# Exchange between partition quarters on VectorE, slice 13's cast on ACT, and VectorE's work that waits for ACT behind the gap's lower part

## Chip, cores and metric

One core of a Trainium2 chip. The metric is the device time of one execution in microseconds, the median of several. A profile is of one execution; its span runs from the first to the last instruction.

## What is computed

Agent attention and then a gated feed-forward layer, all in float32, B = 4, N = 12480 tokens, C = 128 channels, 49 agents, 2048 hidden columns:

```python
def sm(a, b):
    s = scale * (a @ b.transpose(0, 2, 1))      # scale = 1 / sqrt(128)
    e = np.exp(s - s.max(-1, keepdims=True))
    return e / (e.sum(-1, keepdims=True) + 1e-09)
agent_v = sm(agents, k) @ v
x = (sm(q, agents) @ agent_v).reshape(B * N, C)
h = x @ w_in
out = (h * (1.0 / (1.0 + np.exp(-1.702 * h)))) @ w_out
```

## The kernel before

**Groups, slices, gaps.** The tokens are cut into 52 groups of 960 (n = 0 to 51, 13 to a batch, two halves of 480), the hidden columns into 16 slices of 128. For a group n and a slice f (u = 16 n + f) the kernel does: `up`, products of the query weights (agent values times w_in) into two PSUM banks `ph`; ACT's gelu of both halves into `g`; `high`, g rounded to float32r, `gh`; `low`, VectorE's gl = g - gh; `down`, three products of (gh, gl) with the high and low part of w_out, added up in two banks `po`. Products are done in pairs, one on the upper and one on the lower 64 rows of the array.

**The cast in `high`** has two makers (`by_dma`): for even slices and those in `BY_DMA` a DMA that POOL issues, one gap later (`late`); for the others ACT, at the end of the same gap (`soon`). `low` runs three slices behind `up`; `down` of slice f stands in the group's own gaps f and f + 1, five and six gaps behind its `up`. There are 5 buffers of g, 7 of gh and 5 of gl, and 4 banks of `ph`, so two slices.

**The order by hand.** The whole program is a list of gaps, 17 to a group (`GAPS`), written out in `gap`: first the jobs put at that gap, then `up` of one slice, `low` of the slice three back, the `down` products, and last the `high` of the slices that are due. Gap k of group n holds `up` of slice k - 1 + 6 counted from group n, so the group's own slices 6 to 15 go up in its gaps 1 to 10 and the next group's 0 to 5 in gaps 11 to 16. Each engine runs its instructions in this order; a job put at a gap stands in front of that gap's `low` on VectorE and of its gelu on ACT.

**Jobs.** Beside the feed-forward work of one batch run the next batch's keys, then its values, then its weights, and always the query attention of the groups ahead. Key scores of a slice of keys take two gaps from the places in `K_AT` (even groups 2, 8, 14; odd groups 4, 11), values one gap from `V_AT` (even 6, 13; odd 3, 9, 15). All of these and the query scores share one tile of two banks, `ps_m`. Two gaps behind the key scores `key_store` has ACT copy one part of the banks to `score`, VectorE add the other to it and VectorE take the running maximum. A value tile is cast to `v_pair` by a DMA that POOL issues (`value_high`), five gaps ahead of its product.

**Query softmax.** The scores of two groups lie in `e` as blocks of 32 agents by tokens, with the 49 agents in two neighbouring quarters of the partitions. So the maximum (`query_max`) and the sum (`query_sums`) of a quarter have to be joined with those of its neighbour: `exchange` makes four copies of 32 x 30 from `m` or `z` to `x`, each to the other quarter. The one of maxima is put at gap 7 of an even group, after `query_max` at 5 and before `query_shift` at 12; the one of sums at gap 4 of the odd group, before `query_recip` at 6. `query_back` writes p at gaps 6 and 12, `query_high` (ACT, q_hi) and `query_low` (VectorE, q_lo = p - q_hi) follow at 9 and 15.

**What shares what.** POOL's queue holds the exchanges, the gh casts and the v_pair casts; SP's queue the loads (keys, values, queries) and the stores. VectorE's order in a gap is jobs, then `low`.

Of the kernel before, what the change touches and what calls it, by code (L numbers as in the profile page):

```python
# [18 lines left out]
TB = 120  # L19
KB = 8  # L20
# [7 lines left out]
GAPS = 17  # L28
E_AT = 0
BL = 32  # L30
A0 = 25
K_AT = ((2, 8, 14), (4, 11))
V_AT = ((6, 13), (3, 9, 15))
PAIR = 2 * 128 + 16
BY_DMA = (5, 13)
EARLY = 3
EPS = 1e-09

# [2 lines left out]
def kernel(  # L41
# [10 lines left out]
    nc = tc.nc  # L52
# [225 lines left out]
    def by_bank(t):  # L278
        return t.rearrange("p (c j) a -> p c j a", c=2)
# [29 lines left out]

    def key_store(g, s):  # L310
        out = by_bank(score[:TB, g * KB : (g + 1) * KB, :])
        if isinstance(s, tuple):
            nc.scalar.copy(out=out, in_=s[0])  # L313
            nc.vector.tensor_add(out=out, in0=s[1], in1=out)  # L314
            s = out
        else:
            nc.scalar.copy(out=out, in_=s)
        running_max(g, s)

    def key_max_0(d):  # L320
# [361 lines left out]
            scores_exact(b, kts.pop((b, g)), columns(banks[b, g][0]))  # L682

    def do_key_store(b, g):
        key_store(g, banks.pop((b, g))[1])

    def do_key_values(b, g):
        sums[b, g] = key_values(g)
# [15 lines left out]
    def do_query_max(k):  # L704
        tops[k] = query_max(k)
        others[k] = small("x")

    def do_exchange(k, of, quarters, by):
        exchange(of[k], others[k], quarters, by)

    def do_query_shift(k):
        query_shift(k, tops.pop(k), others.pop(k))
# [193 lines left out]
    def put(t, fn):  # L906
        at.setdefault(t, []).append(fn)
# [12 lines left out]
    for n in range(B * NG):  # L920
        t = LAG + n * GAPS
        m = n + 1
        runs = [(t, n + 3)] if n else [(t + 3, 2), (t + 11, 3)]
        for at_, q in runs:
            if q < B * NG:
                take(at_, 1)
                put(at_, lambda q=q: do_query_scores(q))
                put(at_ + 1, lambda q=q: do_query_turn(q))
            if q > 2:
                put(at_ + 2, lambda q=q: do_query_load(q + 1))  # L930
        k = n // 2 + 1
        if n % 2 == 0 and k < B * NG // 2:
            put(t + (5 if n else 13), lambda k=k: do_query_max(k))
            put(t + (12 if n else 15), lambda k=k: do_query_shift(k))
            put(t + GAPS, lambda k=k: query_exp(k))
            put(t + GAPS + 2, lambda k=k: do_query_sums(k))
            put(t + GAPS + 6, lambda k=k: do_query_recip(k))
            for i in range(2):
                quarters = (2 * i, 2 * i + 1)
                put(t + (7 if n else 14), lambda k=k, q=quarters: do_exchange(k, tops, q, nc.gpsimd.tensor_copy))  # L940
                put(t + GAPS + 4, lambda k=k, q=quarters: do_exchange(k, sums, q, nc.gpsimd.tensor_copy))
                put(t + GAPS + (6, 12)[i], lambda k=k, i=i: do_query_back(k, i))
                put(t + GAPS + (9, 15)[i], lambda m=n + 2 + i: do_query_high(m))
                put(t + GAPS + (9, 15)[i], lambda m=n + 2 + i: do_query_low(m))
    put(0, lambda: do_query_load(3))
    put(LAG + 1, lambda: do_query_back(0, 1))
    put(LAG + 3, lambda: do_query_high(1))
# [22 lines left out]
    for b in range(B - 1):  # L970
        begin = gap_of(b * NG * NF) + (0 if b else 7)
        end = gap_of((b + 1) * NG * NF)
        slots = [LAG + n * GAPS + k for n in range(B * NG) for k in K_AT[n % 2]]
        slots = [t for t in slots if t >= begin + 4][:NKG]
        if not b:
            exact.update(((1, 0), (1, 1)))
        for k, t in enumerate(slots):
            if (b + 1, k) not in exact:
                wide.add((b + 1, k))
            put(max(t - 13, first_free[k] if k < 3 and not b else 0), lambda b=b, k=k: do_key_load(b + 1, k))  # L980
            for i in range(4):
                put(t - 4 + i, lambda b=b, k=k, i=i: do_key_split(b + 1, k, i))
            take(t, 2)
            put(t, lambda b=b, k=k: do_key_scores(b + 1, k, 0))
            put(t + 1, lambda b=b, k=k: do_key_scores(b + 1, k, 1))
            put(t + 2, lambda b=b, k=k: do_key_store(b + 1, k))
        mx = {}
        put(t + 2, lambda mx=mx: key_max_0(mx))
        t = free(t + 3)
        put(t, lambda mx=mx: key_max_1(mx))  # L990
        t = free(t + 2)
        put(t, lambda mx=mx: key_max_2(mx))
        shift = t + 1

        n0 = (shift + 1 - LAG - E_AT + GAPS - 1) // GAPS
        places = [(n, i) for n in range(n0, B * NG) for i in V_AT[n % 2] if i > 5 or n > n0]
        for k, (n, i) in enumerate(places[:NKG]):
            t = LAG + n * GAPS + i
            exp_at = LAG + (n if i > 5 else n - 1) * GAPS + E_AT
            exps.setdefault(exp_at, []).append(k)  # L1000
            put(min(shift + 3 * k, exp_at - 1), lambda k=k: key_shift(k, nc.vector.tensor_tensor))
            put(t - 16, lambda b=b, k=k: do_value_load(b + 1, k))
            put(t - 5, lambda b=b, k=k: value_high(vts[b + 1, k]))
            put(t - 2, lambda b=b, k=k: value_low(vts.pop((b + 1, k))))
            put(t - 4, lambda k=k: key_pair(k))
            take(t, 1)
            put(t, lambda b=b, k=k: do_key_values(b + 1, k))
            put(t + 1, lambda b=b, k=k: do_key_sum(b + 1, k))
        w = {}
        put(t + 2, lambda b=b, w=w: weights_0(accs.pop(b + 1), w))  # L1010
        t = free(t + 3)
        put(t, lambda w=w: weights_1(w))
        for c in range(0, F // 512, 2):
            t = free(t + 2)
            assert t < end + 4 * c - 3, (b, begin, shift, end, t)
            put(t, lambda b=b, w=w, c=c: weights_parts(b + 1, w, c))
# [43 lines left out]
    def gap(t):  # L1060
        n, k = divmod(t - LAG, GAPS)
        final = n == B * NG - 1
        if t < LAG:
            u = t if t < LAG - 1 else None
        elif final:
            u = n * NF + LAG + k
        elif k == 0:
            u = LAG - 1 if n == 0 else None
        else:
            u = n * NF + LAG + k - 1  # L1070
        before, late[:] = list(late), []
        rest()
        for job in at.pop(t, ()):
            job()
        if u is not None:
            if u < total:
                do_up(u)
                rest()
            if k != NF:
                for i in low_of(u):  # L1080
                    do_low(i)
        if t >= LAG:
            do_downs(n, k)
        if u is not None and k == NF:
            for i in low_of(u):
                do_low(i)
        for u in before + soon:
            do_high(u)
        soon.clear()
        if k == 2 or final:  # L1090
            send()
# [57 lines left out]
```

## Time and profile before

| | |
|---|---|
| median of 3 runs | 1913.1 us (1912.54 to 1915.93) |
| the profiled execution | 1913.12 us |
| its span | 1911.3 us |
| PE busy | 1877.3 us (98%) |
| VectorE (DVE) busy | 1452.1 us (76%) |
| ACT busy | 1369.4 us (72%) |
| POOL busy | 455.1 us (24%) |
| mean granted TensorE clock | 0.997 |

Busy time is the time in which an engine has an instruction running. PE's matmuls are pipelined and their ends are modelled, so a PE that is busy 98% need not be at its peak; a stop shows better in the distance between the starts of two products. The other engines' shares are means over stages that differ: keys, values and weights come in turn, and in the last 14 groups there is nothing of them. So the rows below are taken by group.

### The profile page before, as it was taken

The page shows a single profiled execution, that of the slowest core. Times are in us where ns is not written, and L with a number is a line of the kernel's source. Part 1 is how long each engine was busy: PE and PEld are TensorE (multiplying, and loading weights), DVE is VectorE, ACT ScalarE, POOL GpSimd, SP SyncE. Part 2 cuts the span into 40 slices and gives each one's busy share as a digit, 9 for nine tenths or more (in the row PEclk, how much of TensorE's full clock was granted, in tenths as well). Part 3 has the DMA queues.
Part 4 walks back from the last instruction along what each step waited for, and adds up shares of the span by engine and source line. Part 5 has one row for each costly group of instructions (what it writes and reads, how often), then busy time and mean ns, then how long its engine had stood idle before and what let it go on. Part 6 is the DMA issues. An engine that isn't in the chain of part 4 may idle for free.

```text
span 1911.3 us, 46738 instructions
## 1 busy us (share of the span) xinstructions
PE 1877.3 (98%) x18872; PEld 1666.2 (87%) x18872; DVE 1452.1 (76%) x1826; ACT 1369.4 (72%) x2314; POOL 455.1 (24%) x822
## 2 busy tenths in 40 slices
PE   8999999999999999999999999999999999999999
PEld 8699988888888998887888999988888888898897
DVE  7888788787678887886877887787876666676664
ACT  4677677777676677776776776866767777777775
POOL 0113323223223212222212232232221122212111
PEclk9999999999999999999999999999999999999999
DMA  9465558788556556887755554888974545555444
GB/s 366 165 218 200 193 176 238 223 236 219 175 188 207 197 177 207 222 251 215 213 185 186 200 197 167 229 215 208 240 195 166 193 171 190 183 175 186 161 167 151
DMA packets 158979, 384.63 MB, mean 201 GB/s; under 512 B 15699, under 2 KB 73235, under 8 KB 158763
## 3 DMA queue, kind: packets, MB, share of 16 engines
q0 software_dynamic: 115152, 273.82, 46.2%
q1 hardware_dynamic: 43611, 107.83, 17.7%
q8 instruction: 148, 2.42, 0.6%
q14 instruction: 68, 0.56, 0.1%
HBM read 82.25 MB, written 25.56 MB: 56 GB/s over the span
## 4 chain that ended last, share of the span: by engine, by line
PE 84%; issue 5%; DVE 5%; DMA 4%; POOL 2%; ACT 1%; POOLq 0%; DVEq 0%; SPq 0%
PE po L216 50%; PE ph L216 26%; PE ps_m L216 4%; DMA gh<-g 3%; PE ps_m L470 2%; DVE gl L592 1%; PE ph L292 1%; POOL x L494 1%; PE ps_m L428 1%; PE po L614 0%; ACT g L573 0%; DVE rest L197 0%; POOL gh L585 0%; DVE score L355 0%; DVE m L503 0%
## 5 line engine op out<-in xcount | busy, mean ns | idle before, releaser
L573 ACT ACTIVATE g<-ph 128x480 f32<-128x480 f32 x1664 | 853.7, 570 | 468.9 <-PE ph L216 414.1
L592 DVE TENSOR_TENSOR gl<-g,gh 128x960 fp32r<-128x960 f32 x832 | 936.7, 1150 | 220.7 <-DMA gh<-g 165.3
L216 PE MATMUL po<-gh,wo_h 64*128 64x480 f32 x3300 | 722.4, 381 | 4.7 <-DMA gh<-g 2.5
L216 PE MATMUL po<-gl,wo_h 64*128 64x480 f32 x3300 | 715.1, 379 | 7.3 <-DVE gl L592 7.2
L216 PE MATMUL po<-gh,wo_l 64*128 64x480 f32 x3300 | 708.1, 375 | 0.0
L585 POOL DMA_DIRECT2D gh<-g x518 | 276.8, 534 | 1358.4 <-ACT g L573 1106.6
L216 PEld LDWEIGHTS po<-gh,wo_h 64*128 64x128 f32 x3300 | 388.3, 184 | 55.4 <-ACT o L622 25.1
L216 PEld LDWEIGHTS po<-gl,wo_h 64*128 64x128 f32 x3300 | 388.5, 186 | 37.7 <-DVE gl L592 12.4
L216 PEld LDWEIGHTS po<-gh,wo_l 64*128 64x128 f32 x3300 | 387.5, 184 | 25.7
L216 PE MATMUL ph<-q_hi,wh 56*128 56x480 f32 x1664 | 369.8, 391 | 0.4 <-ACT wh L433 0.3
L216 PE MATMUL ph<-q_lo,wh 56*128 56x480 f32 x1664 | 359.2, 378 | 0.0
L216 PE MATMUL ph<-q_hi,wl 56*128 56x480 f32 x1664 | 358.1, 377 | 0.3 <-DVE wl L434 0.3
L587 ACT CAST gh<-g 128x960 fp32r<-128x960 f32 x311 | 310.4, 998 | 9.8
L216 PEld LDWEIGHTS ph<-q_hi,wh 56*128 56x128 f32 x1664 | 196.0, 184 | 25.8 <-ACT g L573 5.8
L216 PEld LDWEIGHTS ph<-q_hi,wl 56*128 56x128 f32 x1664 | 195.2, 185 | 14.2 <-DVE wl L434 1.0
L216 PEld LDWEIGHTS ph<-q_lo,wh 56*128 56x128 f32 x1664 | 197.1, 187 | 10.4
L494 POOL COPY x<-m 32x30 f32<-32x30 f32 x100 | 90.6, 906 | 33.0 <-DVE m L503 29.3
L314 DVE TENSOR_TENSOR score<-ps_m,score 120x392 f32<-120x392 f32 x37 | 20.9, 564 | 69.7 <-ACT score L313 62.6
L548 DVE TENSOR_TENSOR q_lo<-p,q_hi 120x480 fp32r<-120x480 f32 x52 | 34.2, 657 | 48.3 <-ACT q_hi L542 48.3
L216 PE MATMUL ps_m<-ag_part,rest 64*128 64x49 bf16 (+1 forms) x1184 | 59.0, 192 | 4.4 <-DVE rest L197 4.1
L372 DVE TENSOR_TENSOR v_pair<-vt,v_pair 120x1024 fp32r<-120x1024 f32 x39 | 47.4, 1216 | 20.6 <-DMA v_pair<-vt 20.6
L624 DVE COPY o<-po 128x480 f32<-128x480 f32 x37 | 24.3, 657 | 50.9 <-PE po L216 46.6
(136 smaller groups left out, 1288.6 us busy)
## 6 DMA issues: line engine op xcount, KB each, us to landing
gh<-g POOLq DMA_DIRECT2D x518, 480.0 KB, 3.3
kt<-kT SPq DMA_DIRECT2D x52, 480.0 KB, 4.0
outT<-o SPq DMA_DIRECT2D x104, 240.0 KB, 4.2
qt<-qT SPq DMA_DIRECT2D x49, 480.0 KB, 4.4
vt<-v SPq DMA_DIRECT2D x39, 512.0 KB, 6.6
v_pair<-vt POOLq DMA_DIRECT2D x39, 480.0 KB, 6.0
vt<-v SPq DMA_DIRECT2D x13, 480.0 KB, 6.4
words<-w_in SPq DMA_DIRECT2D x4, 512.0 KB, 8.7
```

The lines of the kernel that those rows point to most:

```text
L216: ins = nc.tensor.matmul(tile_position=(c * H, 0), **kw)
L292: nc.tensor.matmul(out=ps[:TB, j * 2 * A : (j + 1) * 2 * A], lhsT=kt[:, c * KB // 2 + j, :], rhs=ag_key.rearrange("p b a -> p (b a)"), sta ...
L314: nc.vector.tensor_add(out=out, in0=s[1], in1=out)
L372: nc.vector.tensor_sub(out=vp[:TB, :, C : 2 * C], in0=vt[:TB], in1=vp[:TB, :, 0:C].bitcast(F32))
L470: nc.tensor.matmul(out=ps[c * H : (c + 1) * H, i * n : (i + 1) * n], lhsT=ag_sb[:, b, :], rhs=x[:, t : t + n], start=True, stop=True, tile ...
L494: by(out=x[to * BL : (to + 1) * BL], in_=t[i * BL : (i + 1) * BL])
L548: nc.vector.tensor_sub(out=q_lo[r], in0=p[r], in1=q_hi[r].bitcast(F32))
L573: nc.scalar.activation(out=g[:, c, :], in_=ph[c][:, :CH], func=AF.Gelu_apprx_sigmoid)
L585: nc.gpsimd.dma_start(out=gh, in_=g)
L587: nc.scalar.copy(out=gh, in_=g)
L592: nc.vector.tensor_sub(out=gl, in0=g, in1=gh.bitcast(F32))
L624: nc.vector.tensor_copy(out=o, in_=po[c][:, :CH])
```

## The change

The four calls of `exchange` for a pair of groups (eight copies) go from POOL's `tensor_copy` to VectorE's. Slice 13 leaves `BY_DMA`, so that ACT casts it. The third place for keys in even groups goes from gap 14 to 13. `key_store` keeps ACT's copy alone; VectorE's add and running maximum go to `key_rest`. A second list of jobs, put at half gaps (t + 0.5), runs behind the gap's `low` and `down`; `key_rest`, the first step of the key maximum and `query_low` are put there. In the even groups `query_max` goes from gap 5 to 4, the exchange of maxima from 7 to 6, `query_shift` from 12 to 9; `query_high` from 9 and 15 to 8 and 14.

```diff
--- before.py
+++ after.py
@@ -29,10 +29,10 @@
 E_AT = 0
 BL = 32
 A0 = 25
-K_AT = ((2, 8, 14), (4, 11))
+K_AT = ((2, 8, 13), (4, 11))
 V_AT = ((6, 13), (3, 9, 15))
 PAIR = 2 * 128 + 16
-BY_DMA = (5, 13)
+BY_DMA = (5,)
 EARLY = 3
 EPS = 1e-09
 
@@ -309,12 +309,13 @@
 
     def key_store(g, s):
         out = by_bank(score[:TB, g * KB : (g + 1) * KB, :])
+        nc.scalar.copy(out=out, in_=s[0] if isinstance(s, tuple) else s)
+
+    def key_rest(g, s):
+        out = by_bank(score[:TB, g * KB : (g + 1) * KB, :])
         if isinstance(s, tuple):
-            nc.scalar.copy(out=out, in_=s[0])
             nc.vector.tensor_add(out=out, in0=s[1], in1=out)
             s = out
-        else:
-            nc.scalar.copy(out=out, in_=s)
         running_max(g, s)
 
     def key_max_0(d):
@@ -682,7 +683,10 @@
             scores_exact(b, kts.pop((b, g)), columns(banks[b, g][0]))
 
     def do_key_store(b, g):
-        key_store(g, banks.pop((b, g))[1])
+        key_store(g, banks[b, g][1])
+
+    def do_key_rest(b, g):
+        key_rest(g, banks.pop((b, g))[1])
 
     def do_key_values(b, g):
         sums[b, g] = key_values(g)
@@ -930,18 +934,18 @@
                 put(at_ + 2, lambda q=q: do_query_load(q + 1))
         k = n // 2 + 1
         if n % 2 == 0 and k < B * NG // 2:
-            put(t + (5 if n else 13), lambda k=k: do_query_max(k))
-            put(t + (12 if n else 15), lambda k=k: do_query_shift(k))
+            put(t + (4 if n else 13), lambda k=k: do_query_max(k))
+            put(t + (9 if n else 15), lambda k=k: do_query_shift(k))
             put(t + GAPS, lambda k=k: query_exp(k))
             put(t + GAPS + 2, lambda k=k: do_query_sums(k))
             put(t + GAPS + 6, lambda k=k: do_query_recip(k))
             for i in range(2):
                 quarters = (2 * i, 2 * i + 1)
-                put(t + (7 if n else 14), lambda k=k, q=quarters: do_exchange(k, tops, q, nc.gpsimd.tensor_copy))
-                put(t + GAPS + 4, lambda k=k, q=quarters: do_exchange(k, sums, q, nc.gpsimd.tensor_copy))
+                put(t + (6 if n else 14), lambda k=k, q=quarters: do_exchange(k, tops, q, nc.vector.tensor_copy))
+                put(t + GAPS + 4, lambda k=k, q=quarters: do_exchange(k, sums, q, nc.vector.tensor_copy))
                 put(t + GAPS + (6, 12)[i], lambda k=k, i=i: do_query_back(k, i))
-                put(t + GAPS + (9, 15)[i], lambda m=n + 2 + i: do_query_high(m))
-                put(t + GAPS + (9, 15)[i], lambda m=n + 2 + i: do_query_low(m))
+                put(t + GAPS + (8, 14)[i], lambda m=n + 2 + i: do_query_high(m))
+                put(t + GAPS + (8.5, 14.5)[i], lambda m=n + 2 + i: do_query_low(m))
     put(0, lambda: do_query_load(3))
     put(LAG + 1, lambda: do_query_back(0, 1))
     put(LAG + 3, lambda: do_query_high(1))
@@ -984,8 +988,9 @@
             put(t, lambda b=b, k=k: do_key_scores(b + 1, k, 0))
             put(t + 1, lambda b=b, k=k: do_key_scores(b + 1, k, 1))
             put(t + 2, lambda b=b, k=k: do_key_store(b + 1, k))
+            put(t + 2.5, lambda b=b, k=k: do_key_rest(b + 1, k))
         mx = {}
-        put(t + 2, lambda mx=mx: key_max_0(mx))
+        put(t + 2.5, lambda mx=mx: key_max_0(mx))
         t = free(t + 3)
         put(t, lambda mx=mx: key_max_1(mx))
         t = free(t + 2)
@@ -1084,6 +1089,8 @@
         if u is not None and k == NF:
             for i in low_of(u):
                 do_low(i)
+        for job in at.pop(t + 0.5, ()):
+            job()
         for u in before + soon:
             do_high(u)
         soon.clear()
```

## Rows read from the trace of the kernel before

**Rows 1.** The page's head line.
```profile
span 1911.3 us, 46738 instructions
```
**Rows 2.** Stretches of one group each: length, busy us (instructions) by engine, clock, DMA; tail, even value, even key, odd value.
```profile
1553.83:1586.53 32.70, 32.70 (x298) 28.01 (x296) 23.73 (x29) 25.91 (x44) 6.41 (x14) 1.00 0.52 182
...
433.39:468.30 34.91, 34.91 (x332) 31.27 (x329) 25.62 (x31) 26.01 (x43) 10.33 (x17) 1.00 0.88 226
864.32:905.16 40.84, 37.62 (x330) 32.41 (x328) 26.55 (x32) 26.02 (x43) 10.33 (x17) 0.96 0.79 219
sum 301.29, PE 288.17 PEld 248.28 DVE 217.50 ACT 208.28 POOL 83.17; mean PE 36.02 PEld 31.03 DVE 27.19 ACT 26.04 POOL 10.40
...
649.48:686.59 37.11, 37.11 (x492) 34.52 (x490) 29.92 (x39) 24.80 (x44) 10.52 (x17) 1.00 0.59 205
212.61:251.22 38.61, 37.18 (x492) 34.61 (x489) 29.88 (x39) 24.75 (x44) 12.65 (x17) 1.00 0.53 184
sum 263.88, PE 260.21 PEld 241.21 DVE 209.05 ACT 173.31 POOL 85.68; mean PE 37.17 PEld 34.46 DVE 29.86 ACT 24.76 POOL 12.24
...
828.76:864.32 35.56, 35.56 (x346) 32.41 (x344) 30.67 (x39) 27.52 (x46) 9.01 (x17) 1.00 0.84 236
sum 215.63, PE 214.56 PEld 194.79 DVE 188.34 ACT 164.97 POOL 55.71; mean PE 35.76 PEld 32.47 DVE 31.39 ACT 27.49 POOL 9.29
```
**Rows 3.** Timeline of PE: start and length in us, operation, count [idle before, releaser].
```profile
372.66 0.49 PE L216 MATMUL po<-gl,wo_h 64*128 64x480 f32 x2 [0.81 <-DVE gl L592]
...
876.77 0.49 PE L216 MATMUL po<-gh,wo_h 64*128 64x480 f32 x2
878.06 0.49 PE L216 MATMUL po<-gl,wo_h 64*128 64x480 f32 x2 [0.80 <-DVE gl L592]
...
889.53 0.39 PE L216 MATMUL po<-gh,wo_l 64*128 64x480 f32 x2
891.05 0.48 PE L216 MATMUL po<-gh,wo_h 64*128 64x480 f32 x2 [1.14 <-DMA gh<-g]
892.35 0.49 PE L216 MATMUL po<-gl,wo_h 64*128 64x480 f32 x2 [0.81 <-DVE gl L592]
...
1393.23 0.49 PE L216 MATMUL po<-gl,wo_h 64*128 64x480 f32 x2 [0.47 <-DVE gl L592]
```
**Rows 4.** A stretch of 2 us, columns as in rows 2: the clock is third from the end.
```profile
895.00:897.00 2.00, 2.00 (x14) 1.93 (x12) 2.00 (x3) 0.74 (x2) 0.00 (x0) 0.50 0.00 0
```
**Rows 5.** Timeline of POOL in groups n = 4 and n = 22.
```profile
224.62 7.20 POOL L494 COPY x<-m 32x30 f32<-32x30 f32 x4
...
878.98 2.58 POOL L494 COPY x<-m 32x30 f32<-32x30 f32 x4 [4.03 <-DVE m L503]
881.51 0.96 POOL L368 DMA_DIRECT2D v_pair<-vt  x1
882.46 1.09 POOL L585 DMA_DIRECT2D gh<-g  x2
```
**Rows 6.** The exchange's copies, whole run: count, ns min/median/max, first and last start.
```profile
L494 POOL COPY x<-m x100: 200/208/6460, 93.2 to 1794.5; 32x30 f32<-32x30 f32 x100
L494 POOL COPY x<-z x100: 200/207/1699, 109.0 to 1820.6; 32x30 f32<-32x30 f32 x100
...
L494 DVE COPY x<-z x4: 170/174/176, 47.4 to 47.9; 32x30 f32<-32x30 f32 x4
```
**Rows 7.** The page's groups: count, busy us, mean ns, idle us before, its releasers.
```profile
L592 DVE TENSOR_TENSOR gl<-g,gh 128x960 fp32r<-128x960 f32 x832 | 936.7, 1150 | 220.7 <-DMA gh<-g 165.3
...
L587 ACT CAST gh<-g 128x960 fp32r<-128x960 f32 x311 | 310.4, 998 | 9.8
...
L314 DVE TENSOR_TENSOR score<-ps_m,score 120x392 f32<-120x392 f32 x37 | 20.9, 564 | 69.7 <-ACT score L313 62.6
```
**Rows 8.** The gh casts that POOL issues, whole run, columns as in rows 6.
```profile
L585 POOL DMA_DIRECT2D gh<-g x518: 528/531/732, 62.2 to 1896.6; - x173
...
DMA to landing us min/median/max: 2.8/3.3/9.8
```

## The prediction

> **What bounds the kernel now.** I read the span first [rows 1], then the stretches of one token group each, then the stops of PE inside them, then what PE's releasers had waited for. In a group of the tail, where neither keys nor values are done beside the feed-forward work, PE is busy for 32.70 of 32.70 us [rows 2]: there it is the bound and nothing else can be late. With work beside it a group has a floor as well, the cheapest group of the same make: 34.91 us for an even group with two value slices, 37.11 for an even one with three key slices, 35.56 for an odd one with three value slices [rows 2]. In these PE is busy throughout too. So all that an edit off PE can win is what groups of the same make take over their floor:
> - eight even value groups (n = 6, 8, 10, 20, 22, 32, 34, 36): 301.29 - 8 x 34.91 = 22.0 us;
> - seven even key groups: 263.88 - 7 x 37.11 = 4.1 us;
> - six odd value groups: 215.63 - 6 x 35.56 = 2.3 us [rows 2].
>
> The dearest is n = 22 with 40.84 us [rows 2]. It has two stops. In the **second**, PE's pair at 889.53 is followed by one at 891.05 that waits for a DMA into gh, and that by one at 892.35 that waits for VectorE's gl [rows 3]; pairs come every 0.22 us when nothing is late (a down product is one such pair), so 1.3 + 1.1 us are lost. Two microseconds later the granted clock is 0.50, which is 1.2 GHz, with PE busy all the while [rows 4]; it had stood still for most of the 2.5 us behind 889.9. The rest of the 5.9 us over the floor is that slower stretch and the slices behind it. Why was gh late? POOL did the exchange x<-m from 878.98 for 2.58 us, then the issue for v_pair at 881.51, and only then two gh casts, at 882.46 [rows 5]: slices 12 and 13, one behind the other. In the key group n = 4 the same exchange took 7.20 us [rows 5]. The copies themselves are short: the median is 208 ns, the longest 6460 ns (x<-m) and 1699 ns (x<-z) [rows 6]. The **first** stop, 876.77 and 878.06 [rows 3], comes before any exchange of its group: gh of slice 6 landed late among query load, output stores and value load. Five of the eight groups have it, from 372.66 to 1393.23 [rows 3]; read like the second one, by the gaps between starts, they cost 1.4, 1.5, 1.3, 0.9 and 1.0 us, 6.1 in all; a small one (0.3 us) lies in the floor group too.
>
> **The change part by part.** *Exchange.* 50 exchanges (25 of x<-m, 25 of x<-z) leave POOL, four copies each. On VectorE one copy takes 174 ns [rows 6], taken as 0.77 us for four with the small gaps between them: 50 x 0.77 = 38.5 us more VectorE time. They lie beside PE's work. The exchange of maxima stands in gap 6 of an even group, ahead of low for slice 8; the one of sums in gap 4 of an odd group, ahead of low for slice 6. VectorE is busy for 217.50 / 8 = 27.2 us of an even value group, 29.9 of the even key floor, 188.34 / 6 = 31.4 of an odd value group [rows 2], so the time is there (32.2 of 35.6 in the tightest). Where VectorE waits for a DMA into gh anyway, the exchange of sums falls into that wait. I take nothing on the path, and 38.5 us as the far bound. What POOL gets back is its place in the queue: slice 12's issue is no longer behind an exchange of 2.6 to 7.2 us, and v_pair's, put at gap 8, is no longer behind it either, so it runs some microseconds before the gh casts and not into them.
>
> *A page against it.* One gh issue took 732 ns where the median is 531 [rows 8]. The Trainium skill (SBUF — State Buffer, Who interferes with whom) says that a VectorE copy in its two-port mode holds the port pair that it shares with GpSimd, and that GpSimd can't write DMA descriptors meanwhile: the four new copies would delay an issue. By the trace that is 0.2 us at most in 518 issues, and by the copies' own length 0.77 us an exchange; against 2.6 to 7.2 us before, the sum stays as it is by either.
>
> *Slice 13 by ACT.* 52 casts of 998 ns [rows 7] are 51.9 us more on ACT, 52 issues of 531 ns [rows 8] less on POOL, and 52 of the 518 gh transfers [rows 8] less. The cast stands at the end of gap 8, behind that slice's two gelus, between the DMA slices 12 and 14. ACT is busy for 27.5 of 35.9 us in the odd value groups [rows 2], so 28.5 fit; in gap 8 of an odd group, with q_hi moved there as well, it has more than a gap's work and is behind by less than 1 us until gap 9, which has one slice's gelus alone. The two slices of ph that PE may run ahead cover that; without them it would be on PE's path. Taken: 0; bounds: 0 and 0.6 us in each of 26 odd groups, 16 us. What it gives back: in the second stop's burst (v_pair, 12, value load, 13, 14) a gh landing took up to 9.8 us against a median of 3.3 [rows 8]; one of five transfers goes, and v_pair moves out in front of it.
>
> *VectorE's work behind the lows.* key_rest and q_low go behind the gap's low. Now VectorE stands before them for ACT, 69.7 us before the key add, most of it for ACT's score copy [rows 7], with a low (1.15 us) queued behind it. What is queued behind the wait afterwards is only the next gap's work. Nothing of this is counted as PE time, since no stop that I read has it as its last cause; it pays for VectorE's new 38.5 us. Who waits: the bank of ps_m is free later, by one low, 1.15 us. Its next taker comes two gaps later or more (key slot 13, store at 15, query scores at 17), 3.9 us: covered. With the slot left at 14 it would not be. key_max_0 moves behind the low too, ahead of a transpose of PE in the next gap, three times in all: between -1 and +1.15 us each, since the low comes before it where the wait for ACT stood; I take 0.
>
> *Earlier places.* Max 5 to 4, shift 12 to 9, q_hi 9 to 8 and 15 to 14: the same instructions; the maximum now comes before low of slice 6, where VectorE waits for that gh in the first stop, so it no longer lies in the catch-up behind it. I count nothing.
>
> **The sum.** The first stops are no work of the change: 22.0 - (6.1 - 5 x 0.3) = 17.4 us can go in even value groups, 4.1 in even key groups (all behind the exchange), 2.3 in odd value groups (gh of slice 8 stood behind x<-z). 17.4 + 4.1 + 2.3 = 23.8. Span 1911.3 - 23.8 = 1887.5; the profiled execution is 1.8 us longer than its span and agrees with the median (1913.12 and 1913.1), so **1889 us**.
>
> **The rivals.**
> *A, the burst stays.* The landing is late for the transfers' own sake, and only POOL's lateness goes: in n = 22 slice 12 is issued about 1.1 us earlier, 7 groups x 1.1 = 7.7, and 4.1 + 2.3 as above: 14.1, hence 1899 us. For it: landings up to 9.8 us [rows 8]. Against it: v_pair leaves the burst, and a transfer with it.
> *B, the first stops go too.* With the maximum ahead of them and less traffic: 6.1 us more, 1883. Against it: nothing that feeds slice 6's transfer changes.
> *C, slower: VectorE's queue.* Place: gaps 4 to 8, where one engine in order has exchange, sums or shift and the lows. PE waits as soon as a low ends later than the start of its gl product; in the odd value groups that is where VectorE already has 31.4 us of work. If every exchange outside the 14 or so of the tail, where VectorE is busy for 23.73 of 32.70 us [rows 2], came onto the path, it were 36 x 0.77 = 27.7 us against 23.8 won: 1917 us. It decides from 31 of these 36 on. Against it: 69.7 us of waiting leave the same queue.
> *D, no change: ps_m.* The stops go, and PE stops instead at the next taker of the bank: 39 slices x 0.6 us (half a low) = 23.4. Against it: the takers lie two gaps away.
>
> **How the numbers follow.** Forecast 0.67, A 0.17, B 0.05, D 0.05, C 0.06. The measurement can tell about 0.2%, 3.8 us. Forecast, A and B are faster: 0.89; same 0.05; slower 0.06. The range takes in forecast, A and B with a margin of 2 us: 1881 to 1901; it leaves C and D out.
>
> **What will show it.** Right, step by step: no COPY on POOL, 208 on VectorE of about 0.17 us; POOL's issue of slice 12 some 0.3 us behind its gelu; 466 gh transfers; n = 22 and n = 32 within 1.5 us of 35 us, no stretch at 0.50 inside; the key group n = 4 at 37.1; VectorE's wait for ACT's score far under 62 us; first stops still there. Wrong if the gap between starts at 889 only shrinks (A), if tail groups leave 32.7 us, if PE waits for VectorE in gaps 4 to 8 of groups that stood at their floor (C), or before query or key scores (D).

## The result and the profile after

The change takes 1890.3 us (median; 1888.5 to 1891.4) against 1914.5 of the kernel before in the same series: 24.2 us less, a ratio of 0.9872 [0.9855, 0.9890]. The forecast was 1889. The profiled execution of after took 1891.41 us, its span is 21.7 us shorter than the one of [rows 1], and PE is busy for 99% of it. Head and first section of its page:

```profile
span 1889.6 us, 46586 instructions
PE 1869.7 (99%) x18872; PEld 1677.2 (89%) x18872; DVE 1490.3 (79%) x2026; ACT 1418.8 (75%) x2366; POOL 293.3 (16%) x570
```

VectorE has 38.2 us more to do and ACT 49.4 us more, POOL 161.8 us less. That answers which engine does the work, not where the time was won. For this the stretches of one group each, as in [rows 2]: length, busy us (instructions) by engine, clock, DMA share, GB/s; a tail group, two even value groups (n = 22 and 32) with the sum of eight, an even key group (n = 4) with the sum of seven, two odd value groups (n = 21 and 23) with the sum of six:

```profile
1532.09:1564.77 32.68, 32.68 (x300) 30.09 (x296) 24.33 (x33) 26.82 (x45) 4.78 (x9) 1.00 0.48 166
...
858.69:893.65 34.96, 34.96 (x330) 30.11 (x328) 27.35 (x36) 26.90 (x44) 7.37 (x12) 1.00 0.85 230
1217.59:1252.48 34.89, 34.89 (x330) 30.66 (x328) 30.02 (x42) 27.01 (x44) 7.31 (x12) 1.00 0.94 227
sum 281.93, PE 279.74 PEld 248.66 DVE 225.44 ACT 215.72 POOL 59.29; mean PE 34.97 PEld 31.08 DVE 28.18 ACT 26.96 POOL 7.41
...
213.99:250.92 36.93, 36.93 (x491) 34.88 (x489) 30.08 (x41) 25.75 (x45) 5.12 (x12) 1.00 0.52 175
sum 258.56, PE 258.56 PEld 239.58 DVE 210.91 ACT 180.30 POOL 35.70; mean PE 36.94 PEld 34.23 DVE 30.13 ACT 25.76 POOL 5.10
...
822.12:858.69 36.57, 36.09 (x347) 33.01 (x345) 31.32 (x43) 28.58 (x47) 7.07 (x12) 1.00 0.87 221
893.65:930.34 36.69, 36.11 (x348) 33.99 (x346) 31.26 (x43) 28.64 (x47) 7.05 (x12) 1.00 0.74 203
sum 216.29, PE 214.84 PEld 198.48 DVE 191.47 ACT 171.26 POOL 41.92; mean PE 35.81 PEld 33.08 DVE 31.91 ACT 28.54 POOL 6.99
```

Against [rows 2] the even value groups lose 301.29 - 281.93 = 19.4 us, the even key groups 5.3; the odd value groups gain 0.7. n = 22 fell from 40.84 to 34.96 us, and its granted clock is 1.00 where it was 0.96. The rest of the span gives back 2.3 us. Most of that is the start, ahead of the first group's turn in this count: 65.28 us against 62.56 of before, in which the clock was low for longer (0.92 against 0.97 on the mean):

```profile
0.00:65.28 65.28, 57.54 (x513) 47.81 (x513) 47.33 (x106) 30.50 (x66) 3.94 (x29) 0.92 0.79 291
```

Over the profiles of all kernels here this start takes 61.1 to 65.4 us (65.28 and 63.07 in two profiles of the change), so it is taken as no part of the change.

POOL's timeline in n = 22 has no copy any more, and each issue stands by itself (compare [rows 5]). The four copies of the exchange are in VectorE's timeline, behind two lows of which the first had waited for a DMA into gh:

```profile
868.76 0.53 POOL L586 DMA_DIRECT2D gh<-g  x1 [2.34 <-ACT g L574]
870.18 0.94 POOL L369 DMA_DIRECT2D v_pair<-vt  x1 [0.88 <-PE ps_m L216]
874.60 0.56 POOL L586 DMA_DIRECT2D gh<-g  x1 [3.48 <-ACT g L574]
...
870.08 2.23 DVE L593 TENSOR_TENSOR gl<-g,gh 128x960 fp32r<-128x960 f32 x2 [3.58 <-DMA gh<-g]
872.33 0.73 DVE L495 COPY x<-m 32x30 f32<-32x30 f32 x4
```

Whole run: the copies (count, ns min/median/max, first and last start), the gh casts that POOL issues with their landing, and the wait of VectorE for ACT's score (us, times, longest):

```profile
L495 DVE COPY x<-m x104: 169/174/280, 41.8 to 1769.6; 32x30 f32<-32x30 f32 x104
...
L586 POOL DMA_DIRECT2D gh<-g x466: 528/531/662, 64.9 to 1874.9; - x156
...
DMA to landing us min/median/max: 2.8/3.1/8.8
...
DVE score L317 <- ACT score L312: 30.2, 13, 3.2
```

### The profile page after: what moved, and what is told of

Read it like the earlier page. It is cut to its first block, busy times and chain, and to the rows that moved or that the text cites. A ratio compares the mean times of both kernels' runs of the same rounds, so it can differ in the third digit from the quotient of the medians.

```text
span 1889.6 us, 46586 instructions
## 1 busy us (share of the span) xinstructions
PE 1869.7 (99%) x18872; PEld 1677.2 (89%) x18872; DVE 1490.3 (79%) x2026; ACT 1418.8 (75%) x2366; POOL 293.3 (16%) x570
## 4 chain that ended last, share of the span: by engine, by line
PE 83%; issue 9%; DVE 4%; DMA 2%; POOL 1%; ACT 0%; POOLq 0%; DVEq 0%
PE po L216 49%; PE ph L216 25%; PE ps_m L216 3%; DMA gh<-g 2%; PE ps_m L471 2%; DVE gl L593 1%; PE ph L292 1%; PE ps_m L429 1%; POOL gh L586 1%; POOL v_pair L369 1%; PE po L615 0%; DVE score L356 0%; DVE v_pair L373 0%; DVE rest L197 0%; ACT g L574 0%
## 5 line engine op out<-in xcount | busy, mean ns | idle before, releaser
L586 POOL DMA_DIRECT2D gh<-g x466 | 248.5, 533 | 1506.9 <-ACT g L574 1193.2
L216 PEld LDWEIGHTS po<-gh,wo_h 64*128 64x128 f32 x3300 | 393.6, 184 | 48.1 <-ACT o L623 24.6
L216 PEld LDWEIGHTS po<-gl,wo_h 64*128 64x128 f32 x3300 | 394.4, 186 | 26.8 <-DVE gl L593 4.3
L216 PEld LDWEIGHTS po<-gh,wo_l 64*128 64x128 f32 x3300 | 393.1, 184 | 23.5
L588 ACT CAST gh<-g 128x960 fp32r<-128x960 f32 x363 | 362.1, 998 | 11.5
L216 PEld LDWEIGHTS ph<-q_hi,wh 56*128 56x128 f32 x1664 | 198.9, 184 | 24.2 <-ACT g L574 5.7
L216 PE MATMUL ps_m<-ag_part,kt 64*128 64x98 bf16 (+1 forms) x1184 | 59.9, 195 | 0.0
L373 DVE TENSOR_TENSOR v_pair<-vt,v_pair 120x1024 fp32r<-120x1024 f32 x39 | 47.5, 1217 | 14.9 <-DMA v_pair<-vt 14.7
L216 PEld LDWEIGHTS <-kt 64*128 64x128 bf16 x1184 | 49.3, 93 | 11.0 <-issue 6.9
L216 PE MATMUL ps_m<-ag_part,rest 64*128 64x98 bf16 (+1 forms) x1184 | 57.6, 192 | 1.1 <-DVE rest L197 0.9
L216 PEld LDWEIGHTS <-rest 64*128 64x128 bf16 x1184 | 51.8, 94 | 1.4 <-DVE rest L197 1.4
```

The source lines that it names most:

```text
L216: ins = nc.tensor.matmul(tile_position=(c * H, 0), **kw)
L373: nc.vector.tensor_sub(out=vp[:TB, :, C : 2 * C], in0=vt[:TB], in1=vp[:TB, :, 0:C].bitcast(F32))
L586: nc.gpsimd.dma_start(out=gh, in_=g)
L588: nc.scalar.copy(out=gh, in_=g)
```

## The experiments

Theory T is the prediction's: the exchange in POOL's queue makes slice 12's cast late, and taking it out of there is the gain. Its rivals: R1, slice 13's transfer in the same burst is the cause; R2, VectorE's waits for ACT are; R3, the *places* of the steps are enough, whatever the engine. The expectations call T theory Q or rival E (the copies must leave POOL), R1 rival A, R2 rival V and R3 theory Q2; Q3 splits Q2 into two causes. All ratios are to the kernel before on the same chip; sums are those of eight even value, seven even key and six odd value groups in the profiled execution (before: 301.29 / 263.88 / 215.63; change: 281.93 / 258.56 / 216.29).

### Each part alone

**Exchange on VectorE, at the old places.**

```diff
-put(t + (7 if n else 14), ... do_exchange(k, tops, q, nc.gpsimd.tensor_copy))
-put(t + GAPS + 4, ... do_exchange(k, sums, q, nc.gpsimd.tensor_copy))
+put(t + (7 if n else 14), ... do_exchange(k, tops, q, nc.vector.tensor_copy))
+put(t + GAPS + 4, ... do_exchange(k, sums, q, nc.vector.tensor_copy))
```

> The kernel before with one edit: all four copies of each exchange on VectorE, at their old places; slice 13 stays with the DMA. Theory Q (PE's stops come from the exchange standing in POOL's queue ahead of v_pair and slices 12 and 13): about 21 us faster than before, ratio 0.989, even value groups together near 283 us (301.3 before), even key groups near 260 (263.9). Rival A (the burst of transfers makes the landings late): about 14 us faster, ratio 0.993, second stops in n = 22 and n = 32 still over 1.5 us. Rival V (VectorE's waits for ACT ahead of the lows are what counts): no change, or slower by the 38.5 us of copies that VectorE gets.

Measured: 1897.2 us, 0.9917 [0.9891, 0.9944]; sums 281.40 / 266.90 / 214.71. The even value groups win all that the change wins there, but the even key groups get *dearer* by 3.0 us, while the whole change makes them 5.3 cheaper. n = 4 of this run, the sums of both kinds, and two rows of PE's waits (us, times, longest):

```profile
214.91:252.89 37.98, 37.34 (x491) 34.43 (x488) 30.49 (x43) 24.74 (x44) 5.63 (x13) 1.00 0.53 188
...
sum 281.40, PE 280.18 PEld 247.18 DVE 225.07 ACT 208.24 POOL 62.90; mean PE 35.02 PEld 30.90 DVE 28.13 ACT 26.03 POOL 7.86
...
sum 266.90, PE 261.66 PEld 237.18 DVE 213.83 ACT 173.24 POOL 39.28; mean PE 37.38 PEld 33.88 DVE 30.55 ACT 24.75 POOL 5.61
...
PEld L216 <- DVE rest L197: 7.1, 15, 0.8
PE ps_m L216 <- DVE rest L197: 4.9, 10, 0.7
```

`rest` is the last split piece of the keys, needed by the key scores at gap 8; the four copies at gap 7 stand ahead of it in VectorE's queue (VectorE in n = 4 of this run, then the PE product that waits):

```profile
229.54 0.73 DVE L494 COPY x<-m 32x30 f32<-32x30 f32 x4
230.31 0.69 DVE L197 TENSOR_TENSOR rest<-rest 128x480 bf16<-128x480 f32 x1
...
231.06 0.20 PE L216 MATMUL ps_m<-ag_part,rest 64*128 64x49 bf16 x1 [0.58 <-DVE rest L197]
```

Their 0.7 us show in six of the seven groups, which take 37.90 to 37.99 us, as 0.8 to 0.9 us over the floor of 37.11. In the kernel before, the second of these waits came 5 times for 4.1 us, in the change twice for 0.9. So the move alone removes the second stops, and pays for it elsewhere; the expectation had the even key groups near 260.

**Slice 13 cast by ACT, nothing else.**

```diff
-BY_DMA = (5, 13)
+BY_DMA = (5,)
```

> The kernel before with one edit: slice 13 cast by ACT in every group; the exchange stays on POOL. Theory Q: slice 12 is still issued 1.4 to 4.1 us late, but nothing waits for slice 13: the even key groups' stops go (4 us), those of the even value groups by about half (9 us): ratio 0.993. Rival A: one of five transfers of the burst less, the landings come back towards 4 us and nearly all second stops go: ratio 0.989. Rival V: no change.

Measured: 1918.3 us, 1.0023 [1.0000, 1.0047]; sums 306.49 / 262.18 / 215.54. One transfer fewer in the burst removes no stop: R1 falls.

**Half gaps only** (`key_rest`, the first step of the key maximum and `query_low` behind the gap's low).

```diff
-put(t + GAPS + (9, 15)[i], lambda m=n + 2 + i: do_query_low(m))
+put(t + GAPS + (9.5, 15.5)[i], lambda m=n + 2 + i: do_query_low(m))
+put(t + 2.5, lambda b=b, k=k: do_key_rest(b + 1, k))
-put(t + 2, lambda mx=mx: key_max_0(mx))
+put(t + 2.5, lambda mx=mx: key_max_0(mx))
```

> The kernel before with one edit: key_rest, the first step of the key maximum and q_low behind the gap's low, all other places as before. Theory Q and rival A: no change, within 0.2% (ratio 0.998 to 1.002), with VectorE's wait for ACT's score copy falling from 62.6 us to under 35. Rival V: 10 us or more faster, ratio under 0.995. With the third key slice still at gap 14 PE may wait before the query scores for the bank: then up to 0.6 us in each of 7 groups, 4 us slower.

Measured: 1912.9 us, 1.0017 [0.9994, 1.0040]; sums 293.78 / 264.97 / 214.97. The profiled execution was one of the shorter of its kernel; the median shows no gain, though VectorE's wait for ACT's score is down to 14.9 us. R2 falls.

### The places alone

**The change with its copies back on POOL.**

```diff
-put(t + (6 if n else 14), ... do_exchange(k, tops, q, nc.vector.tensor_copy))
-put(t + GAPS + 4, ... do_exchange(k, sums, q, nc.vector.tensor_copy))
+put(t + (6 if n else 14), ... do_exchange(k, tops, q, nc.gpsimd.tensor_copy))
+put(t + GAPS + 4, ... do_exchange(k, sums, q, nc.gpsimd.tensor_copy))
```

> The changed kernel with one edit undone: the exchange's copies are back on POOL, at the new places (gap 6 and gap 4). Theory Q: the copies stand ahead of v_pair and slice 12 again and take 2 to 7 us: half of the gain is lost, ratio to the kernel before 0.993. Rival A: slice 13's transfer stays away, so most of the gain stays: 0.989. Rival V: 0.987 as with the change.

Measured: 1892.0 us, 0.9889 [0.9867, 0.9912]; sums 284.90 / 258.39 / 214.82. Nearly the whole gain stays with the exchange on POOL. T as it was put had half of it go (0.993).

**The kernel before with the new places only**, POOL's copies kept.

```diff
-put(t + (5 if n else 13), lambda k=k: do_query_max(k))
-put(t + (12 if n else 15), lambda k=k: do_query_shift(k))
+put(t + (4 if n else 13), lambda k=k: do_query_max(k))
+put(t + (9 if n else 15), lambda k=k: do_query_shift(k))
-put(t + (7 if n else 14), ... do_exchange(k, tops, q, nc.gpsimd.tensor_copy))
+put(t + (6 if n else 14), ... do_exchange(k, tops, q, nc.gpsimd.tensor_copy))
```

> The kernel before with one edit: the earlier places of the even groups' softmax (maximum at gap 4, exchange at 6, shift at 9); the copies stay on POOL, slice 13 stays with the DMA, nothing goes behind the lows. Theory Q2 (what counts is that the exchange is over before POOL reaches v_pair and slice 12; the engine that makes the copies matters little): the copies of x<-m take under 3 us each time, even value groups fall from 301 to about 285, even key groups from 263.9 to about 260: ratio 0.990. Rival E (the copies must leave POOL): ratio 0.995 to 1.000. Rival V (VectorE's waits count): the added maximum in gap 4 is ahead of a low that has the key store's wait in front of it as well: no gain in key groups.

Measured: 1891.6 us, 0.9901 [0.9885, 0.9917]; sums 281.45 / 258.55 / 219.04. R3 holds: no work changes its engine, and the even value and key groups come out as in the change. The places are enough; as the first experiment shows, for the even value groups the engine is enough too. The odd value groups have one dear member, n = 33 with 39.79 us and a clock of 0.96.

**Of the places, the maximum alone**, from gap 5 to 4. One number of the kernel before is changed:

```diff
-put(t + (5 if n else 13), lambda k=k: do_query_max(k))
+put(t + (4 if n else 13), lambda k=k: do_query_max(k))
```

> The kernel before with one edit: the maximum of the even groups at gap 4 in place of 5; the exchange stays at gap 7 on POOL, the shift at 12. Theory Q3 (two causes: in value groups the maximum came late because it stood behind the low that waits for slice 6; in key groups the copy itself is held up by VectorE's unbroken row of two-input operations from gap 5 on): value groups gain about half or more of their 20 us, even key groups stay at 263 to 265 with copies of 6 us and over: ratio 0.993. Rival (only the wait for the maximum): key groups fall to 259 as well, ratio 0.990. Rival (only the hold-up of copies): nothing changes in either.

Beside it the change itself, once more on this chip:

> The changed kernel itself, on the chip that runs the next three as well, so that they can be set against it: ratio 0.987, even value groups together 280 to 283 us, no clock stretch at half speed outside start and end.

Measured: 1893.9 us, 0.9880 [0.9856, 0.9903], the change 1894.2, 0.9878 [0.9853, 0.9903]; sums 282.42 / 260.61 / 218.37 and 282.32 / 261.76 / 216.28. One number gives what the whole change gives. It is more than Q3 expected (0.993, even key groups at 263 to 265): the rival that looks at the wait for the maximum alone was nearer. The change's two profiles differ by 3.2 us in the even key groups (258.56 and 261.76), so a difference of that size between two single profiles says nothing by itself. Where the edit acts is seen in the exchange's row of the page (count, busy us, mean ns, idle us before, its releaser), first of the kernel before, then of this one:

```profile
L494 POOL COPY x<-m 32x30 f32<-32x30 f32 x100 | 90.6, 906 | 33.0 <-DVE m L503 29.3
```

```profile
L494 POOL COPY x<-m 32x30 f32<-32x30 f32 x100 | 69.0, 690 | 5.6 <-DVE m L503 1.5
```

Before, POOL stood 29.3 us in front of the exchange for VectorE's maximum, now 1.5. VectorE's timeline of the kernel before in n = 22 shows why the maximum was late: it came right behind a low that had waited for its gh.

```profile
876.85 1.16 DVE L592 TENSOR_TENSOR gl<-g,gh 128x960 fp32r<-128x960 f32 x1 [4.67 <-DMA gh<-g]
877.93 0.93 DVE L503 TENSOR_REDUCE m<-e 128x30 f32<-128x750 f32 x1
878.77 2.23 DVE L592 TENSOR_TENSOR gl<-g,gh 128x960 fp32r<-128x960 f32 x2
```

With the maximum a gap earlier it is done 6 us before that low, and POOL goes through exchange and v_pair in one go and then waits for ACT (VectorE and POOL, n = 22 of that kernel):

```profile
863.43 0.93 DVE L503 TENSOR_REDUCE m<-e 128x30 f32<-128x750 f32 x1
...
870.55 3.30 DVE L592 TENSOR_TENSOR gl<-g,gh 128x960 fp32r<-128x960 f32 x3 [3.77 <-PE ph L216]
...
869.36 0.94 POOL L494 COPY x<-m 32x30 f32<-32x30 f32 x4
870.25 0.96 POOL L368 DMA_DIRECT2D v_pair<-vt  x1
875.07 0.56 POOL L585 DMA_DIRECT2D gh<-g  x1 [3.87 <-ACT g L573]
```

### One part undone

**Slice 13 by DMA again**, the rest of the change kept.

```diff
-BY_DMA = (5,)
+BY_DMA = (5, 13)
```

> The changed kernel with one edit undone: slice 13 cast by the DMA again. Theory Q2: with POOL's queue free of the exchange the third transfer is harmless: within 3 us of the changed kernel, ratio to before 0.987 to 0.989. Rival A (the burst): stops at slices 12 to 14 of the even value groups come back, 9 us or more: 0.992.

Measured: 1888.6 us, 0.9891 [0.9872, 0.9910]; sums 279.53 / 259.86 / 214.32. Nothing is lost.

**Without the half gaps.**

```diff
-put(t + GAPS + (8.5, 14.5)[i], lambda m=n + 2 + i: do_query_low(m))
+put(t + GAPS + (8, 14)[i], lambda m=n + 2 + i: do_query_low(m))
-put(t + 2.5, lambda b=b, k=k: do_key_rest(b + 1, k))
+put(t + 2, lambda b=b, k=k: do_key_rest(b + 1, k))
-put(t + 2.5, lambda mx=mx: key_max_0(mx))
+put(t + 2, lambda mx=mx: key_max_0(mx))
```

> The changed kernel with one edit undone: key_rest, the key maximum's first step and q_low stand ahead of the low again (same gaps, half gaps gone). Theory Q2: 0 to 4 us slower than the changed kernel, ratio to before 0.987 to 0.989. Rival V: the gain of the change was the waits of VectorE: half of it is lost or more, 0.993 and up, with stops in front of key scores where a split piece comes late.

Measured: 1890.3 us, 0.9897 [0.9872, 0.9922]; sums 285.17 / 258.53 / 217.80. The sums of the even and odd value groups are 3.2 and 1.5 us up in the profile, which is of the longest of the four executions (1895.5 us); the median is not.

**The third key slot back at gap 14.**

```diff
-K_AT = ((2, 8, 13), (4, 11))
+K_AT = ((2, 8, 14), (4, 11))
```

> The changed kernel with one edit undone: the third key slice of even groups at gap 14 again. If the bank that VectorE's add frees later makes PE wait before the query scores: up to 0.6 us in each of 7 key groups, about 4 us slower than the changed kernel, ratio 0.990, seen as PE waiting in the step after gap 16. If not, only the packing of key scores beside other work differs: within 2 us.

Measured: 1893.7 us, 0.9908 [0.9888, 0.9928]; sums 282.14 / 258.86 / 214.87. None of the seven key groups is dearer in the profile. But n = 0, which the sums leave out, has the stop that was looked for: the query scores wait 1.01 us there and start 0.1 us behind the end of VectorE's running maximum, which reads ps_m (VectorE, then PE; the releaser named on PE's row had long been done):

```profile
101.67 0.56 DVE L308 TENSOR_TENSOR run_max<-ps_m,run_max 120x392 f32<-120x392 f32 x1
...
102.33 1.03 PE L471 MATMUL ps_m<-qt,ag_sb 128*64 128x240 f32 x8 [1.01 <-PE po L216]
```

The run of the half gaps alone, whose slot is at 14 too, has it with 2.10 us in n = 0 and with 0.48 in n = 28; the change has none. The profile is of the shortest of the four executions (1888.5 us; the others took 1893.6 to 1894.4). The interval overlaps those of the two kernels above, which ran on the same chip, so what the slot costs in the median stays open.

### The first stops

They were to stay, and what is left over the floor should be theirs. Slice 6's gh lands late among output stores, query and value loads. So the stores of the group before are sent at gap 5 instead of 2, in the change:

```diff
-        if k == 2 or final:
+        if k == 5 or final:
             send()
```

> The changed kernel with one edit: the output stores are sent at gap 5 in place of gap 2. Theory: the first stops come from the transfers that run beside slice 6's (query load, two stores, value load): with the stores out of the way the landing of slice 6 falls by about 1 us and the first stops left (5 us in all) go: ratio 0.985. Rival (slice 6 waits for the value load and v_pair alone, or the stores then meet slices 8 and 10): no change, or stops move to the odd groups.

Measured: 1884.5 us, 0.9832 [0.9803, 0.9860]; sums 277.79 / 258.84 / 214.00. The sum of the even value groups:

```profile
sum 277.79, PE 277.79 PEld 256.89 DVE 224.34 ACT 215.81 POOL 58.96; mean PE 34.72 PEld 32.11 DVE 28.04 ACT 26.98 POOL 7.37
```

PE is busy for all of it; the eight groups lie between 34.58 and 34.80 us. Slice 6's gh now lands 5.3 to 6.8 us after its issue in them, where it took 5.9 to 8.8 in the change: 1.1 us less on the mean, as the theory said. So 277.79 is taken as the floor of this make. Seen from it the kernel before had 23.5 us to lose, the change took 19.4, and 4.1 were left to the first stops.

**The same with slice 13 by DMA.**

```diff
-BY_DMA = (5,)
+BY_DMA = (5, 13)
```

> The changed kernel with the stores at gap 5 and slice 13 cast by the DMA again. If slice 13's cast by ACT is worth nothing once the exchange is early: as fast as the kernel with the stores at gap 5 alone, within 3 us; if the burst matters it is 4 us or more slower.

Measured: 1884.0 us, 0.9827 [0.9798, 0.9855]; sums 277.72 / 258.35 / 214.33. The shortest median of all, by 0.5 us, within the spread: with no stop left in the even value groups, slice 13's maker makes no difference to the time.

## Why the prediction was right, and where it was not

**What bounds the kernel, and how much an edit can win: right.** PE does: in the floor groups it is busy throughout, as before. They have moved down a little: 34.64 us is now the cheapest even value group (34.91 before), 36.82 the cheapest even key group (37.11).

**Even value groups, 17.4 us forecast, 19.4 measured.** No even value group has a second stop any more. n = 22 and n = 32 take 34.96 and 34.89 us. The 2.0 us more are a part of the first stops, taken as untouched: of some 6 us 4.1 are left. Five groups still show one, the dearest n = 8 (36.85 us).

**The slow clock behind a stop: right.** n = 22's stretch at 0.50 [rows 4] is gone together with the stop ahead of it, as is the one of n = 32 (both groups had a mean of 0.96 before and have 1.00 now).

**Even key groups, 4.1 forecast, 5.3 measured (2.1 in the change's second profile).** Forecast was a return to the floor of 37.11. n = 4 went from 38.61 to 36.93: its stop is gone, and the floor itself moved by some 0.2 us. It did so with the new places alone too (258.55), and with the slot at 14 (258.86), but not with the maximum alone (n = 4 at 37.18), so the new places of exchange and shift are enough for it. The forecast put these stops "behind the exchange" and did not say where PE stops. In n = 4 it is not at a down product but at key scores. POOL's exchange of 7.20 us makes the casts behind it late, VectorE's low waits for one of them, `rest` stands behind that low, and PE waits for `rest` (VectorE, then PE, kernel before):

```profile
238.17 1.16 DVE L592 TENSOR_TENSOR gl<-g,gh 128x960 fp32r<-128x960 f32 x1 [1.34 <-DMA gh<-g]
...
241.96 0.69 DVE L197 TENSOR_TENSOR rest<-rest 128x480 bf16<-128x480 f32 x1
...
242.71 0.20 PE L216 MATMUL ps_m<-ag_part,rest 64*128 64x49 bf16 x1 [1.43 <-DVE rest L197]
```

**Odd value groups, 2.3 forecast, -0.7 measured: mis-sized.** The mechanism (slice 8's cast behind the exchange of sums) shows in two groups: n = 7 and n = 9 fell from 36.15 and 36.14 us to 35.55 and 35.54. They take 35.54 to 35.78 in the eight profiles with the copies on VectorE and 35.75 to 36.36 in the six with POOL's; slice 8 of n = 7 is issued 1.0 to 1.2 us behind its gelu in the six, 0.29 in the eight. But n = 21 and n = 23 are 1 us dearer. VectorE's timeline of the change in n = 21:

```profile
829.64 0.77 DVE L495 COPY x<-z 32x30 f32<-32x30 f32 x4
...
832.62 1.16 DVE L593 TENSOR_TENSOR gl<-g,gh 128x960 fp32r<-128x960 f32 x1 [1.47 <-DMA gh<-g]
```

The exchange is done 2.2 us before that low starts, and the low waits for its gh, not for the copies. That landing took 5.7 us here where it took 3.3 before. The change makes the even group ahead shorter, and what that group sends and loads is closer to this slice's transfer: a reason that was only argued. Over all kernels the sum lies between 214.00 and 219.04 and goes neither with the exchange's engine (214.71 and 216.29 on VectorE) nor with slice 13; n = 21 is dear (36.35 to 36.66) in both profiles of the change and without the half gaps, and takes 35.56 to 35.72 in all others. Which group gets a late landing stays open. The two kernels that have an early maximum, POOL's copies and slice 13 by DMA both had n = 33 at 39.5 us or more, and no other kernel had. In both, POOL issued slice 8 of n = 33 behind an exchange of sums of 2.57 us and a v_pair, 2.1 and 2.4 us behind its gelu, and it landed after 7.1 and 7.3 us (0.3 to 1.2, and 4.3 to 6.4, in the others). So there the copies on POOL do cost; why only in these two was not settled.

**The exchange as the cause: half right, and this is the step that failed.** The item on the earlier places ("I count nothing") is the wrong one. The forecast itself noted that the maximum would no longer lie in the catch-up behind the first stop, and gave it no price. But [rows 5] has it: the exchange's row ends in 4.03 us of waiting for VectorE's maximum. The chain runs from a DMA over VectorE and POOL back to a DMA: gh of slice 6 lands late (first stop); VectorE's low for it waits at the head of its queue; the maximum, which needs nothing of that slice, stands behind it; POOL's exchange waits for the maximum, and v_pair and the casts of slices 12 and 13 behind the exchange; gh of slice 12 is late (second stop). It can be cut in two places. Taking the exchange off POOL cuts it at the end and costs 3.0 us in the key groups at the old places; putting the maximum ahead of the low cuts it at the beginning, at no cost in the even groups. Either makes the even value groups 281 to 282 us, and both together the same: the parts are alternatives and don't add up. The change does both, so the sum came out right with a cause that was only one of two. That the groups' terms, off by +2.0, +1.2 and -3.0 us, add up to 24.0 against 23.8 is luck.

**Exchange on VectorE, nothing on the path: right in the change, by its place.** 174 ns a copy as forecast, and 38.2 us more VectorE work, on no path. At gap 7 it would have cost 0.8 us in an even key group (the first experiment): rival C's mechanism, at a place that C didn't name. At gap 6 it is out of the way in the profile shown, but not always: in the change's second profile PE waits for `rest` five times, 2.1 us in all, and in n = 4 the four copies (0.73 us) stand ahead of `rest` again, behind a low that had waited 2.77 us for its gh (1.74 in the first profile). What part the copies have in that wait was not separated.

**Slice 13 by ACT, cost 0 of 0 to 16: right, and so is its use.** 466 transfers, the median landing 3.1 against 3.3 us. It neither costs nor gives anything measurable in the time, alone or undone. (Alone, n = 4 and n = 14 stood at their floor, 37.18 and 37.10 us, but other key groups did not.)

**Work behind the lows: 0, right.** VectorE's wait for ACT's score fell from 62.6 to 30.2 us, and neither alone nor undone does that show in the time. The reason given for moving the key slot ("with the slot left at 14 it would not be") holds, but rarely: with the slot at 14 the bank stopped PE once in one profile (1.01 us) and twice in another (2.10 and 0.48 us), in no more than one of the seven key groups.

**Slice 12's issue.** It was to come 0.3 us behind its gelu, and comes 0.29 behind in all eight groups, where it was 1.2 to 1.6 before; its landing takes 2.8 to 3.8 us, where it took 5.2 to 8.6. So the larger part of what came back lies in the landing, not in the issue. What goes with it is v_pair. Before, v_pair is issued 0.95 us ahead of slice 12 in all eight groups, and lands 4.1 to 6.0 us after slice 12's issue; in the change it is issued 3.5 to 5.8 us ahead and lands at most 1.9 us after it: "some microseconds before the gh casts and not into them", as the forecast had it. The landings of v_pair and of slice 12 in n = 22, issued at 881.51 and 882.46 before, at 870.18 and 874.60 after:

```profile
DMA to landing us min/median/max: 5.6/5.6/5.6
DMA to landing us min/median/max: 8.6/8.6/8.6
...
DMA to landing us min/median/max: 5.0/5.0/5.0
DMA to landing us min/median/max: 2.9/2.9/2.9
```

It goes this way through all 14 profiles: the three kernels that win nothing (before, slice 13 alone, half gaps alone) have v_pair 0.94 to 0.95 us ahead in every even value group and a landing of 5.2 to 9.4 us; all others have it 1.19 us or more ahead, slice 12 issued 0.29 us behind its gelu, and a landing of 2.8 to 6.5. A late issue by itself can be free: with the maximum alone moved, slice 12 of n = 4, a group without v_pair, was issued 3.25 us behind its gelu, landed after 2.8 us, and the group stood at its floor. That the two transfers hold each other up is argued from this; no run moved v_pair alone.

**POOL's issues beside VectorE's copies.** That VectorE's copies would hold up POOL's issues was priced at 0.2 us at most: the longest of 466 issues took 662 ns, 131 over the median.

**The rivals.** A (the burst stays): no, v_pair left it and the landings fell; with the transfer of slice 13 back in the burst the sum is still 279.53. B (first stops go too): a third of them did; the rest went with the stores. C: above. D (ps_m): no such wait in the change; with the slot at 14 it comes up once or twice in a run.

What stays open: whether the differences among the change and its versions with one part undone (1888.6 to 1893.7 us, intervals overlapping) are real. An exchange by ACT was not tried, nor v_pair at an earlier gap with all else as before.

## What to carry to other kernels

Where a step on one engine makes another late, ask first what that step itself had waited for, and whether that is only something ahead of it in an in-order queue: putting it one place ahead of the waiting instruction may give all that moving it to another engine gives. Parts of a change that cut the same chain don't add up, so price them as alternatives and look for the cheapest. The floor of groups of the same make tells how much is left and, here, that a shift of three gaps in when the stores are sent was worth another 0.5%.

## What the runs showed of the hardware

**A copy of 0.2 us can take 6.5 on POOL while VectorE works.** In the kernel before the four copies of n = 4 ran from 224.62 for 7.20 us [rows 5], one of them for 6460 ns [rows 6]. VectorE's timeline there is a row without a break, every instruction of it with two inputs in SBUF:

```profile
224.42 1.15 DVE L592 TENSOR_TENSOR gl<-g,gh 128x960 fp32r<-128x960 f32 x1
225.48 0.66 DVE L195 TENSOR_TENSOR rest<-kt 128x480 f32<-128x480 f32 x1
226.05 1.16 DVE L592 TENSOR_TENSOR gl<-g,gh 128x960 fp32r<-128x960 f32 x1
227.12 0.72 DVE L197 TENSOR_TENSOR rest<-rest 128x480 bf16<-128x480 f32 x1
227.73 3.29 DVE L592 TENSOR_TENSOR gl<-g,gh 128x960 fp32r<-128x960 f32 x3
```

It ends at 231.02, and the slow copy at 231.1. The Trainium skill (SBUF — State Buffer, Who interferes with whom) says that a VectorE instruction with two SBUF inputs contends with a GpSimd instruction that reads SBUF, and that the later of the two is blocked until the other is done. The trace agrees for one instruction and shows more: the copy did not get in between the seven instructions of the row either. With the exchange at gap 6 on POOL the longest copy of maxima took 1273 ns. By itself the hold-up need not cost anything: with only the maximum moved, the exchange of n = 4 still took 6.37 us, and the group 37.18, its floor. That the contention is the cause of the hold-up is read from the times, not shown by a run made for it.

```profile
227.37 6.37 POOL L494 COPY x<-m 32x30 f32<-32x30 f32 x4
```
